# Weight steps in pairs, a shorter centroid chain and a fused softplus end, in another order of issue: clustered attention and a softplus FFN on one core

## The chip, the core and the metric

The kernel runs on one core of one Trainium2 chip. Time is device microseconds (us) of one execution. Before the change three runs gave 818.27, 818.87 and 819.67, so the median is 818.87.

## What is computed

```python
q_assign = np.argmax(np.einsum('bhsd,hcd->bhsc', q_n, c_n), axis=-1)   # nearest of 16 centroids
k_assign = np.argmax(np.einsum('bhsd,hcd->bhsc', k_n, c_n), axis=-1)
mask = q_assign[:, :, :, None] == k_assign[:, :, None, :]
scores = np.where(mask, scale * np.matmul(q, k.transpose(0, 1, 3, 2)), -1000000000.0)
attn = softmax(scores)                     # max, exp, sum, division
x = (attn @ v) as (B * S, H * D)
h = x @ w_in
g = np.maximum(h, 0.0) + np.log1p(np.exp(-np.abs(h)))
return g @ w_out
```

Four batches, 8 heads, 768 positions of 64 numbers; the FFN takes 3072 tokens of 512 through 2048. The weights and the centroids are scaled up by a constant factor. `w_in` and `w_out` come as 64-bit floats; q, k, v and the centroids as 32-bit floats.

## The kernel before

The precision is that of 32-bit floats, and the matrix products run in 16-bit floats: each operand is split in a high part (a cast) and a low part (a subtraction), and three products are added. So nearly every tile passes through a cast and a subtraction on one of three engines: ACT, DVE or POOL.

The work stands in 192 score tiles of 128 queries by 768 keys, numbered t, in eight passes `pi` of 24 tiles (half a batch each). For a tile, `scores(t)` (L1084 on) issues four matmuls into one of two `s` buffers, the row maximum on DVE (L1116), the exponential on ACT (L1125), then cast (L579) and subtraction (L561) into `phl`, and a DMA that transposes a pair of tiles into `pt` (`flip`). The first 24 tiles are transposed by PE instead, in full precision (L1142), since the path by DMA has not started by then. `attend(t)` (L1238, L1242, L1243) multiplies `pt` by v. When all heads of a pass are attended, `ffn1(pi, f)` computes 16 tiles `h` (L1330 to L1332) for that pass, `softplus(pi, f)` turns each of them into g, and `ffn2` multiplies by `w_out` (L1418 to L1420).

`softplus` has five operations for each h: |h| with a sign (L1357 on DVE or L1361 on ACT), max(h, 0) (L1368 or L1369), exp (L1374), log (L1375), and the sum (L1379 on DVE or POOL). The PSUM bank of `h` is given back after the second. Three banks are shared by h (two at most), o (two at most) and x.

`prep_weights(step)` turns 64-bit weights into the two 16-bit parts in 32 steps of 128 by 512, 16 for `w_in` and 16 for `w_out`: a load into a free part of `wo`, a scaling (L707 to L709, on ACT, DVE or POOL), the low bits (L724, L725), two joins on DVE (L736, L742), a cast and a subtraction. `prep_centroids` normalizes the centroids in a chain of small operations (L618 to L639), mostly on DVE, which ends in three transposes on PE and a copy (L644, L647); the first assignment of keys waits for it.

Everything is issued in an order that is written down: `SEQUENCE` names at each position the chain whose next operation is issued, and, by its thousands, on which of the engines open to it. Each engine runs its instructions in that order. Small matmuls on constant data (`warm`, L526) fill places where PE is expected to wait; how many there are is computed from the planner's own costs.

Of the kernel before, what the change touches and what calls it, by code (L numbers as in the profile page):

```python
# [8 lines left out]
F16 = mybir.dt.float16  # L9
# [10 lines left out]
SW2 = 256.0  # L20
# [9 lines left out]
PSC = 1560  # L30
PQS = 1950
# [9 lines left out]
WARM_FROM = 600  # L41
WARM_SHARE = 0.65
# [6 lines left out]
TURN = "...e.t.t................"  # L49
CAPS = {"h": 2, "o": 2, "x": 3}  # L50
# [54 lines left out]
]  # L105
SEQUENCE = [
# [172 lines left out]
class Order:  # L279
# [7 lines left out]
    PIPE = {"PE": 0, "DVE": 82, "ACT": 105, "POOL": 43, "SP": 0}  # L287

    def __init__(self):
        self.free = {"PE": 1800.0, "DVE": 2500.0, "ACT": 2000.0, "POOL": 2700.0, "SP": 1000.0}  # L290
        self.ev, self.blocked, self.active = {}, {}, {}
        self.dma = 0.0
        self.loads = 0
# [117 lines left out]
    def run(self):  # L411
        for code in SEQUENCE:
# [6 lines left out]
            if eng == "PE" and self.warm:  # L419
                self.warm(self.free["PE"], start)  # L420
# [1101 lines left out]
```

## Time and profile before

| | us |
|---|---|
| runs: lowest, median, highest | 818.27, 818.87, 819.67 |
| span of the profiled execution, first to last instruction | 816.3 |
| PE busy | 801.5 (98%) |
| DVE busy | 653.4 (80%) |
| ACT busy | 603.3 (74%) |
| POOL busy | 446.3 (55%) |

Of the profiled execution the page gives the span, which leaves out the launch ahead of the first instruction and what follows the last one; the median of the runs is 2.6 us above it. PE is the TensorE matmul, DVE is VectorE, ACT is ScalarE, POOL is GpSimd; SP issues the DMAs. Busy time is the union of an engine's instructions. Matmuls overlap in the pipeline, so that a short wait of PE can be hidden in its busy time.

### The profile page before, as it was taken

The numbers are of one execution on the slowest core, as the hardware profiler recorded it, in microseconds if no ns is written. First come the engines' busy times: TensorE is split into PE (matmuls) and PEld (weight loads), VectorE is DVE, ScalarE is ACT, GpSimd is POOL, SyncE is SP. The second block draws the span as 40 slices with busy tenths as digits, with TensorE's granted clock in tenths as the row PEclk, the third lists the DMA queues.
The fourth block names the chain that finished last, engine by engine and source line by source line (L and its number), as shares of the span: only waits on it lengthen the run. The fifth ranks groups of instructions, "written<-read, shape, count | busy, mean of one in ns | idle before, by whom it ended". The sixth has DMA issues, their size and how long they took to land.

```text
span 816.3 us, 17689 instructions
## 1 busy us (share of the span) xinstructions
PE 801.5 (98%) x6851; PEld 510.7 (63%) x6851; DVE 653.4 (80%) x1205; ACT 603.3 (74%) x1175; POOL 446.3 (55%) x365
## 2 busy tenths in 40 slices
PE   8999989999999999999999999999999999999998
PEld 8898756665666666665666656656666666555554
DVE  8999999999887887988788898898797877543232
ACT  7999999998777788786777677766787775534330
POOL 4336464565467568675573575765655685432330
DMA  9436999999979999999989799999999777520001
GB/s 331 156 91 158 224 209 255 187 204 215 207 166 166 185 203 204 191 218 180 185 168 179 144 197 181 196 197 188 185 171 164 142 133 140 119 53 14 26 1 39
DMA packets 386451, 134.15 MB, mean 164 GB/s; under 512 B 362688, under 2 KB 379328, under 8 KB 386368
## 3 DMA queue, kind: packets, MB, share of 16 engines
q1 hardware_dynamic: 386368, 133.03, 80.4%
q8 instruction: 53, 0.87, 0.4%
q14 instruction: 30, 0.25, 0.1%
HBM read 35.68 MB, written 6.29 MB: 51 GB/s over the span
## 4 chain that ended last, share of the span: by engine, by line
PE 77%; DMA 7%; DVE 5%; ACT 5%; issue 3%; POOL 2%; SPq 0%; POOLq 0%; ACTq 0%; DVEq 0%
PE s L1100 11%; PE o L1418 9%; PE o L1420 9%; PE o L1419 9%; PE h L1330 9%; PE h L1332 9%; PE h L1331 9%; PE mbank L1242 6%; DMA pt<-phl 5%; PE mbank L1243 3%; PE mbank L1238 2%; ACT p L1125 2%; DVE negm L1116 2%; PE pT L1142 1%; POOL phl L561 1%
## 5 line engine op out<-in xcount | busy, mean ns | idle before, releaser
L1125 ACT ACTIVATE p<-s,negm 128x768 f32<-128x768 f32 x190 | 171.3, 903 | 65.1 <-DVE negm L1116 48.9
L1116 DVE TENSOR_REDUCE negm<-s 128x1 f32<-128x768 f32 x192 | 180.8, 948 | 22.2 <-PE s L1100 21.2
L561 POOL TENSOR_TENSOR phl<-p,phl 128x768 f16<-128x768 f32 x86 | 142.9, 1666 | 76.8 <-ACT phl L579 46.9
L1330 PE MATMUL h<-xT,wi 128*128 128x384 f16 x512 | 166.9, 326 | 0.4 <-ACT fg L1369 0.4
L1332 PE MATMUL h<-xT,wi 128*128 128x384 f16 x512 | 166.9, 326 | 0.0
L1331 PE MATMUL h<-xT,wi 128*128 128x384 f16 x512 | 166.9, 326 | 0.0
L1100 PE MATMUL s<-kt,qt 128*128 128x384 f16 x768 | 155.8, 326 | 2.8 <-ACT p L1125 1.5
L1418 PE MATMUL o<-wo,gh 128*128 128x512 f16 (+2 forms) x392 | 146.5, 375 | 0.8 <-DVE ot L1444 0.6
L1420 PE MATMUL o<-wo,gh 128*128 128x512 f16 (+2 forms) x392 | 146.5, 375 | 0.0
L1419 PE MATMUL o<-wo,gh 128*128 128x512 f16 (+2 forms) x392 | 146.5, 375 | 0.0
L1379 POOL TENSOR_TENSOR fg<-fg,fa 128x384 f32<-128x384 f32 x72 | 77.2, 1074 | 84.4 <-ACT fa L1375 64.4
L1242 PE MATMUL mbank<-vb,pt 128*128 128x128 f16 x1008 | 107.4, 220 | 2.7 <-DVE negm L1116 1.3
L1243 PE MATMUL mbank<-vb,pt 128*128 128x64 f16 x1008 | 103.1, 193 | 0.0
L1100 PEld LDWEIGHTS <-qt 128*128 128x128 f16 x768 | 71.3, 98 | 49.0 <-issue 4.9
L1242 PEld LDWEIGHTS <-pt 128*128 128x128 f16 x1008 | 89.6, 98 | 16.6 <-DMA pt<-phl 4.7
L579 ACT CAST phl<-p 128x768 f16<-128x768 f32 x112 | 91.5, 829 | 11.3 <-DMA pt<-phl 8.3
L1361 ACT ACTIVATE fa<-h 128x384 f32<-128x384 f32 x93 | 45.4, 489 | 70.1 <-PE h L1332 54.0
L1243 PEld LDWEIGHTS <-pt 128*128 128x128 f16 x1008 | 87.6, 98 | 11.4
L561 DVE TENSOR_TENSOR phl<-p,phl 128x768 f16<-128x768 f32 x76 | 81.5, 1078 | 3.0 <-ACT phl L579 2.3
L561 POOL TENSOR_TENSOR gh<-fg,gh 128x768 f16<-128x768 f32 x38 | 65.7, 1728 | 17.0 <-DVE gh L579 7.7
L1332 PEld LDWEIGHTS <-wi 128*128 128x128 f16 x512 | 50.1, 98 | 33.2
L1331 PEld LDWEIGHTS <-wi 128*128 128x128 f16 x512 | 50.1, 98 | 32.4 <-issue 0.5
(182 smaller groups left out, 1388.6 us busy)
## 6 DMA issues: line engine op xcount, KB each, us to landing
wo<-in_moe_w_in_dram SPq DMA_DIRECT2D x16, 512.0 KB, 6.4
wo<-in_moe_w_out_dram SPq DMA_DIRECT2D x14, 512.0 KB, 4.4
rawk<-in_k_dram SPq DMA_DIRECT2D x16, 384.0 KB, 4.3
rawq<-in_q_dram SPq DMA_DIRECT2D x16, 384.0 KB, 4.3
rawv<-in_v_dram SPq DMA_DIRECT2D x16, 384.0 KB, 4.3
out_dram<-ot SPq DMA_DIRECT2D x23, 256.0 KB, 2.4
pt<-phl SPq DMA_TRANSPOSE x82, 5.9
wraw<-in_moe_w_out_dram SPq DMA_DIRECT2D x2, 512.0 KB, 4.6
```

The lines of the kernel that those rows point to most:

```text
L561: [lambda e=e: e.tensor_tensor(dst, a, b, ALU.subtract) for e in (nc.gpsimd, nc.vector)],
L1100: nc.tensor.matmul(st[:, j, :SH], qt[:, s, i], kt[:, s, NT // 2 * j : NT // 2 * (j + 1)], start=(s == 0), stop=(s == 1),)
L1116: yield op("DVE", 950, lambda: nc.vector.tensor_reduce(negm, st[:, :, :SH], AX.XY, ALU.max, negate=True))
L1125: yield op("ACT", 1000, lambda: nc.scalar.activation(ex, st[:, :, :SH], AF.Exp, bias=negm, accum_out=total))
L1242: nc.tensor.matmul(av, pt[:, 0, c], vb[:, c, : 2 * D], start=(c == 0), stop=False)
L1243: nc.tensor.matmul(av[:, D:], pt[:, 1, c], vb[:, c, D : 2 * D], start=False, stop=(c == NT - 1))
L1330: nc.tensor.matmul(hp, w[0], x[0], start=(c == 0), stop=False)
L1331: nc.tensor.matmul(hp, w[0], x[1], start=False, stop=False)
L1332: nc.tensor.matmul(hp, w[1], x[0], start=False, stop=(c == NP - 1))
L1418: nc.tensor.matmul(out_, g[0], wo[:, f, 0, 0, side], start=(f == f0), stop=False)
L1419: nc.tensor.matmul(out_, g[0], wo[:, f, 0, 1, side], start=False, stop=False)
L1420: nc.tensor.matmul(out_, g[1], wo[:, f, 0, 0, side], start=False, stop=(f == f0 + NF // 2 - 1))
```

## The change

- Weight steps: 14 pairs of steps (all of `w_in`, twelve of `w_out`) work on 128 by 1024 at a time; four single steps of `w_out` stay. `wi` is laid out so that the two parts of a pair lie side by side. The rooms into which raw weights are loaded are given out in pairs.
- The scaling on POOL has a second operand (`1.0, mult, mult`) in place of `None`, here and at `prep_q`; the planner's cost for it is lower (`PSC`, `PQS`).
- Centroids: squares and their sum in one ACT instruction, one round of Newton's step for the square root in place of two, the 0.5 and the 1e-6 in one instruction, the two copies in one and the two differences in one, the clearing of `cb` on a chain of its own.
- `FUSED = 2`: in the first two passes max(h, 0) and the sum are one DVE instruction that reads `h` from PSUM after the log; `h`'s bank is given back after it.
- Half of the `ot` scalings may go to ACT; banks are picked from the front of the list of idle ones.
- Fillers stand in a table (`FILLS`, 149 of them, all within the first 171 positions of the order) in place of the computed ones (206).
- Another `SEQUENCE` and other ranks.

```diff
-PSC = 1560
-PQS = 1950
+PSC = 660
+PQS = 920
...
+FUSED = 2
...
+FILLS = {
+    11: 33, 18: 10, 28: 14, 36: 10, 46: 3, 50: 2, 64: 10, 87: 11, 88: 6, 100: 4, 113: 5, 117: 11, 120: 10, 141: 7,
+    159: 6, 165: 3, 170: 4,
+}
+
 SEQUENCE = [
-    0, 0, 0, 0, 0, 0, 0, 0, 0, 0, 1, 2, 4, 0, 1, 0, 6, 468, 469, 1001, 0, 468, 0, 0, 3, 1, 468, 2004, 1, 0, 468, 1,
...
-        bank = min(self.idle, key=self.ev.get)
+        bank = self.idle[0]
...
-            if eng == "PE" and self.warm:
-                self.warm(self.free["PE"], start)
+            if at in FILLS:
+                self.warm(FILLS[at])
...
+    def warm(count):
+        for _ in range(count):
+            nc.tensor.matmul(idle, eye, ones[:, :WARM], start=True, stop=True)
...
-        yield either(300, 250, lambda e: e.tensor_tensor(sq, cf, cf, ALU.mult))
-        yield dve(lambda: V.tensor_reduce(ss, sq, AX.X, ALU.add))
-        yield dve(lambda: V.tensor_scalar(sg, ss, 1e-30, None, ALU.max))
-        yield op("ACT", 200, lambda: nc.scalar.activation(nrm, sg, AF.Ln))
-        yield op("ACT", 200, lambda: nc.scalar.activation(nrm, nrm, AF.Exp, scale=0.5))
-        for _ in range(2):
...
+        yield op("ACT", 370, lambda: nc.scalar.activation(sq, cf, AF.Square, accum_out=ss))
+        yield op("ACT", 200, lambda: nc.scalar.activation(nrm, ss, AF.Ln, bias=tiny))
+        yield op("ACT", 200, lambda: nc.scalar.activation(nrm, nrm, AF.Exp, scale=0.5))
+        yield dve(lambda: V.reciprocal(rn, nrm))
+        yield dve(lambda: V.scalar_tensor_tensor(nrm, rn, ss, nrm, ALU.mult, ALU.add))
+        yield dve(lambda: V.tensor_scalar(nrm, nrm, 0.5, 1e-6, ALU.mult, ALU.add))
+        yield dve(lambda: V.reciprocal(rn, nrm))
+        yield dve(lambda: V.tensor_scalar(cn, cf, rn, None, ALU.mult), 235, shared=True)
...
-    wi = cpool.tile([P, DM // P, DFF // WC, 2, WC], F16, name="wi")
+    wi = cpool.tile([P, DFF // WC, DM // P, 2, WC], F16, name="wi")
...
+    groups = [(s, 2) for s in range(0, NWI + 12, 2)] + [(s, 1) for s in range(NWI + 12, NWI + NF)]
...
-            (660, 420, PSC),
+            (240 + 435 * n, 145 + 275 * n, 130 + 530 * n),
...
-                lambda: nc.gpsimd.tensor_scalar(mag, val, sc, None, ALU.mult),
+                lambda: nc.gpsimd.tensor_scalar(mag, val, sc, 1.0, ALU.mult, ALU.mult),
...
-        yield op("DVE", 685, join, shared=True)
+        yield op("DVE", 151 + 534 * n, join, shared=True)
...
+        fused = pi < FUSED
+        if not fused:
+            yield op(
+                ("DVE", "ACT"),
...
+            od.drop(hk)
         yield op("ACT", 520, lambda: nc.scalar.activation(a, a, AF.Exp, scale=sign[0]))
         yield op("ACT", 520, lambda: nc.scalar.activation(a, a, AF.Ln, bias=1.0))
...
+        if fused:
+            yield op("DVE", 560, lambda: nc.vector.scalar_tensor_tensor(g[:, f % 2], hp, 0.0, a, ALU.max, ALU.add))
+            od.drop(hk)
+        else:
...
```

What the order makes of it is shown at two places. The first is the start of DVE, from the first instruction on the centroids on (`css` is the sum of squares, `cnrm` the norm, `crn` its inverse, `cb` the copies for the transposes, `kn` and `qn` the split keys and queries). Before:

```order
L618 TENSOR_TENSOR csq<-cf 128x64
L619 TENSOR_REDUCE css<-csq 128x1
L620 TENSOR_SCALAR csg<-css 128x1
L624 RECIPROCAL crn<-cnrm 128x1
L625 SCALAR_TENSOR_TENSOR cnrm<-crn,csg,cnrm 128x1
L626 TENSOR_SCALAR cnrm<-cnrm 128x1
L624 RECIPROCAL crn<-cnrm 128x1
L625 SCALAR_TENSOR_TENSOR cnrm<-crn,csg,cnrm 128x1
L626 TENSOR_SCALAR cnrm<-cnrm 128x1
L627 TENSOR_SCALAR cnrm<-cnrm 128x1
L561 TENSOR_TENSOR kn_0_141<-rawk_120,kn_0_141 128x12x64
L628 RECIPROCAL crn<-cnrm 128x1
```

And in the changed kernel, DVE from the same place:

```order
L625 RECIPROCAL crn<-cnrm 128x1
L626 SCALAR_TENSOR_TENSOR cnrm<-crn,css,cnrm 128x1
L627 TENSOR_SCALAR cnrm<-cnrm 128x1
L628 RECIPROCAL crn<-cnrm 128x1
L629 TENSOR_SCALAR cn<-cf,crn 128x64
L634 CAST cb<-cn 128x128
L635 TENSOR_TENSOR cb<-cn,cb 128x2x64
L553 TENSOR_TENSOR kn_0_182<-rawk_123,kn_0_182 128x12x64
```

Seven small instructions now make the whole chain on DVE, and it ends ahead of the first subtraction for the keys; before, that subtraction and two others stood inside it.

The second place is ACT at the first h tile, `h_0`, of the first pass (`fa` holds |h| and then the log, `fg` holds g, `s` and `phl` are score tiles). Before:

```order
L1361 ACTIVATE fa_0_1951<-h_0_1937 128x384
L725 ACTIVATE wo<-wo,down 128x512
L1369 ACTIVATE fg_0_1952<-h_0_1937 128x384
L1374 ACTIVATE fa_0_1951<-fa_0_1951 128x384
L1187 CAST phl_3_1989<-s_3_1830 128x768
L1375 ACTIVATE fa_0_1951<-fa_0_1951 128x384
L579 CAST wo<-wo 128x512
L1187 CAST phl_3_1989<-s_4_1909 128x768
L579 CAST wo<-wo 128x512
```

In the changed kernel, ACT from the first tile's exp on, and DVE from its |h| on:

```order
L1377 ACTIVATE fa_0_1804<-fa_0_1804 128x384
L1378 ACTIVATE fa_0_1804<-fa_0_1804 128x384
L1362 ACTIVATE fa_1_1878<-h_1_1806 128x384
L1377 ACTIVATE fa_1_1878<-fa_1_1878 128x384
L1127 ACTIVATE p_2_5_1869,sum_1_1738<-s_5_1854,negm_5_1863 128x768
L1378 ACTIVATE fa_1_1878<-fa_1_1878 128x384
```

```order
L1358 TENSOR_SCALAR fa_0_1804<-h_0_1779 128x384
L1046 TENSOR_REDUCE aq_1_1848<-sim_q_1_1639 128x12
L1261 TENSOR_REDUCE x_0_1_1772<-mbank 128x128
L1190 TENSOR_TENSOR phl_3_1815<-s_4_1781,phl_3_1815 128x768
L1118 TENSOR_REDUCE negm_5_1863<-s_5_1854 128x1
L1380 SCALAR_TENSOR_TENSOR fg_0_1805<-h_0_1779,fa_0_1804 128x384
```

Exp and log now follow each other on ACT, max(h, 0) is gone from it, and the weight steps' instructions no longer stand among them; on DVE the one fused instruction comes five places behind the |h|.

## Rows read from the trace of the kernel before

**Rows 1.** The page: span, and busy us (share of span) xinstructions of each engine.

```profile
span 816.3 us, 17689 instructions
PE 801.5 (98%) x6851; PEld 510.7 (63%) x6851; DVE 653.4 (80%) x1205; ACT 603.3 (74%) x1175; POOL 446.3 (55%) x365
```

**Rows 2.** Stretches: length, busy PE, PEld, DVE, ACT, POOL; PE clock, DMA share, GB/s.

```profile
0.00:21.70 21.70, 18.57 (x354) 17.82 (x355) 18.14 (x77) 17.40 (x29) 10.63 (x18) 1.00 0.93 337
21.70:88.00 66.30, 65.15 (x653) 57.32 (x651) 65.62 (x135) 65.75 (x137) 30.32 (x30) 1.00 0.51 143
88.00:147.00 59.00, 53.68 (x505) 38.02 (x504) 57.50 (x102) 58.38 (x115) 30.77 (x25) 1.00 1.06 219
147.00:816.00 669.00, 664.13 (x5345) 397.58 (x5345) 512.16 (x895) 461.80 (x898) 374.57 (x293) 1.00 0.81 156
```

**Rows 3.** Groups by line and form: the fillers in 21.7 to 88 and in 88 to 147.

```profile
L526 PE MATMUL mbank<-ones,eye 128*128 128x120 f16 x40 | 3.1, 216 | 0.0
...
L526 PE MATMUL fill<-ones,eye 128*128 128x120 f16 x29 | 2.0, 216 | 0.0
```

**Rows 4.** Waits of PE and its weight loads in 88 to 147: us, times, longest.

```profile
PE s L1100 <- ACT p L1125: 1.3, 3, 0.8
...
PEld L1242 <- DMA pt<-phl: 1.7, 1, 1.7
```

**Rows 5.** Timeline of the opening: first, last DVE instruction on centroids, and ACT's copy.

```profile
2.69 0.23 DVE L618 TENSOR_TENSOR csq<-cf 128x64 f32<-128x64 f32 x1 [0.91 <-DMA cf<-in_centroids_dram]
...
8.91 0.21 DVE L639 TENSOR_TENSOR cb<-cn,cb 128x64 f16<-128x64 f32 x1
...
10.44 0.48 ACT L647 COPY cents<-centsT 128x384 f16<-128x384 f16 x1
```

**Rows 6.** Groups by line and form, whole span: weight steps, and DVE casts of two sizes.

```profile
L736 DVE SCALAR_TENSOR_TENSOR wo<-wo 128x512 int32<-128x512 int32 x30 | 20.5, 700 | 0.5 <-issue 0.4
...
L725 ACT ACTIVATE wo<-wo,down 128x512 int32<-128x512 uint16 x21 | 16.3, 784 | 0.0
...
L579 DVE CAST gh<-fg 128x768 f16<-128x768 f32 x14 | 7.8, 555 | 0.7 <-POOL fg L1379 0.3
...
L579 DVE CAST xn<-x 128x384 f16<-128x384 f32 x10 | 3.7, 365 | 0.2
```

**Rows 7.** The same view: max(h, 0) and the sum in softplus.

```profile
L1379 POOL TENSOR_TENSOR fg<-fg,fa 128x384 f32<-128x384 f32 x72 | 77.2, 1074 | 84.4 <-ACT fa L1375 64.4 <-DVE fg L1368 17.3 <-DVE phl L561 1.7
...
L1369 ACT ACTIVATE fg<-h 128x384 f32<-128x384 f32 x82 | 40.0, 487 | 20.2 <-DVE fa L1357 15.1 <-POOL gh L561 5.1
...
L1379 DVE TENSOR_TENSOR fg<-fg,fa 128x384 f32<-128x384 f32 x56 | 36.3, 652 | 9.3 <-ACT fa L1375 9.1
...
L1368 DVE TENSOR_SCALAR fg<-h 128x384 f32<-128x384 f32 x46 | 25.3, 551 | 13.8 <-ACT fa L1361 11.6 <-POOL gh L561 2.0
```

**Rows 8.** The same view: the low part of a score tile on POOL and on DVE.

```profile
L561 POOL TENSOR_TENSOR phl<-p,phl 128x768 f16<-128x768 f32 x86 | 142.9, 1666 | 76.8 <-ACT phl L579 46.9 <-DVE phl L579 27.6 <-POOL kn L561 0.9
...
L561 DVE TENSOR_TENSOR phl<-p,phl 128x768 f16<-128x768 f32 x76 | 81.5, 1078 | 3.0 <-ACT phl L579 2.3 <-POOL phl L579 0.2
...
L1188 DVE TENSOR_TENSOR phl<-s,phl 128x768 f16<-128x768 f32 x2 | 1.8, 946 | 0.0
```

**Rows 9.** The same view: POOL's cast of weights, and its one scaling with a constant.

```profile
L579 POOL CAST wi<-wo 128x512 f16<-128x512 f32 x5 | 4.0, 801 | 10.0 <-DVE wo L742 8.6 <-ACT ptf L552 1.4
...
L1047 POOL TENSOR_SCALAR n<-n 128x96 f16<-128x96 f16 x2 | 1.2, 582 | 3.1 <-DVE live L1042 3.1
```

**Rows 10.** First h tile's max and sum; PE's waits for h; h's matmuls in 106 to 154.

```profile
109.96 0.48 ACT L1369 ACTIVATE fg<-h 128x384 f32<-128x384 f32 x1
...
114.26 0.99 POOL L1379 TENSOR_TENSOR fg<-fg,fa 128x384 f32<-128x384 f32 x1
...
L1330 PE MATMUL h<-xT,wi 128*128 128x384 f16 x512 | 166.9, 326 | 0.4 <-ACT fg L1369 0.4
...
L1330 PE MATMUL h<-xT,wi x41: 323/326/327, 106.8 to 153.7; 128*128 128x384 f16 x41
```

More of the change, by code (lines that the diff above doesn't have):

```diff
@@ L289, in __init__ @@
     def __init__(self):
-        self.free = {"PE": 1800.0, "DVE": 2500.0, "ACT": 2000.0, "POOL": 2700.0, "SP": 1000.0}
+        self.free = {"PE": 1800.0, "DVE": 2500.0, "ACT": 2650.0, "POOL": 2700.0, "SP": 1000.0}
         self.ev, self.blocked, self.active = {}, {}, {}
@@ L411, in run @@
     def run(self):
-        for code in SEQUENCE:
+        for at, code in enumerate(SEQUENCE):
             which, seq = divmod(code, 1000)
@@ L517, in tile_cluster_attention__then__softplus_ffn @@
     idle = mbank[:, 512 - WARM :]
-    def warm(begin, end):
-        ready, spot = min([(od.ev[b], b[1]) for b in od.idle] + [(od.mread, 9)])
-        gap = end - max(begin, ready)
-        if gap > (150 if begin < 30000 else WARM_FROM):
-            out = idle if spot == 9 else ps_u.tile([P, 512], F32, tag=f"u{spot}", name="fill")[:, :WARM]
-            for _ in range(int(gap * (0.95 if begin < 2500 else 0.75 if begin < 30000 else WARM_SHARE) / (100 if begin < 2500 else 52))):
-                nc.tensor.matmul(out, eye, ones[:, :WARM], start=True, stop=True)
+    def warm(count):
+        for _ in range(count):
+            nc.tensor.matmul(idle, eye, ones[:, :WARM], start=True, stop=True)
     od.warm = warm
@@ L607, in tile_cluster_attention__then__softplus_ffn @@
     cents = cpool.tile([P, 3, H, NCL], F16, name="cents")
+    tiny = cpool.tile([P, 1], F32, name="tiny")
+    nc.vector.memset(tiny, 1e-30)
     def prep_centroids():
         sq = p2.tile([P, D], F32, tag="x320", name="csq", bufs=1)
-        small = [cpool.tile([P, 1], F32, name=f"c{nm}") for nm in ("ss", "sg", "nrm", "rn")]
-        ss, sg, nrm, rn = small
+        small = [cpool.tile([P, 1], F32, name=f"c{nm}") for nm in ("ss", "nrm", "rn")]
+        ss, nrm, rn = small
         V = nc.vector
@@ L631, in prep_centroids, with blank_cb @@
         cn = p2.tile([P, D], F32, name="cn", **own(keys[0], 2))
-        yield dve(lambda: V.tensor_scalar(cn, cf, rn, None, ALU.mult), shared=True)
-        od.set(cf_key)
-        cb = p2.tile([P, 3, 2, D], F16, name="cb", **own(keys[1], 2))
-        yield either(195, 330, lambda e: e.memset(cb, 0.0))
-        for j in range(2):
-            yield either(195, 240, lambda e, j=j: e.tensor_copy(cb[:, 0, j], cn))
-        yield either(195, 290, lambda e: e.tensor_tensor(cb[:, 1, 0], cn, cb[:, 0, 0], ALU.subtract))
-        yield either(195, 290, lambda e: e.tensor_tensor(cb[:, 2, 1], cn, cb[:, 0, 0], ALU.subtract))
+        cb = p2.tile([P, 3, 2, D], F16, name="cb", **own(keys[1], 2))
+        def blank_cb():
+            yield either(195, 330, lambda e: e.memset(cb, 0.0))
+            od.set(("cb",))
+        od.spawn(blank_cb(), od.cur["prio"])
+        yield op("ACT", 370, lambda: nc.scalar.activation(sq, cf, AF.Square, accum_out=ss))
[6 more added lines that the diff above has]
+        yield dve(lambda: V.tensor_scalar(cn, cf, rn, None, ALU.mult), 235, shared=True)
+        od.set(cf_key)
+        both = cn.unsqueeze(1).to_broadcast([P, 2, D])
+        rest = cb.rearrange("p a j d -> p (a j) d")[:, 2:6:3]
+        yield wait("cb")
+        yield either(260, 330, lambda e: e.tensor_copy(cb[:, 0], both))
+        yield either(260, 430, lambda e: e.tensor_tensor(rest, both, cb[:, 0], ALU.subtract))
         hk, ps = yield from bank("x", False, [P, 3, P], F16, "centsT")
@@ L696, in prep_weights @@
         if step:
-            yield wait("wd", step - 1)
-        if f >= 0 and f // 2 in rooms:
-            yield wait("wr", rooms[f // 2])
+            yield wait("wd", groups[gi - 1][0])
+        if f >= 0:
+            for last in sorted({rooms[r] for r in range(f // 2, (f + n - 1) // 2 + 1) if r in rooms}):
+                yield wait("wr", last)
         gate = int(WGATE + step * WPACE)
@@ L744, in prep_weights @@
         )
-        yield cast(part[:, 0], val, WC, WBIAS)
-        yield sub(part[:, 1], val, part[:, 0], WC)
-        od.set(("wr", step))
+        yield cast(part[:, :, 0], val, n * WC, WBIAS)
+        yield sub(part[:, :, 1], val, part[:, :, 0], n * WC)
+        for k in range(n):
+            od.set(("wr", step + k))
         if key:
@@ L1051, in prep_q @@
             ("POOL", "DVE"),
-            (180 + 1290 * part, 130 + DQA * part),
+            (480 + 990 * part, 130 + DQA * part),
             [
@@ L1124, in scores @@
         total = sums[n // 2, pi][:, n % 2 * nt + i]
[L1125 removed]
+        yield op("ACT", 980, lambda: nc.scalar.activation(ex, st[:, :, :SH], AF.Exp, bias=negm, accum_out=total))
         if kind(t) == ".":
@@ L1327, in emit @@
                 for c in range(2 * half, 2 * half + 2):
-                    w = [wi[:, c, f * P // WC, s, w0 : w0 + P] for s in range(2)]
+                    w = [wi[:, f * P // WC, c, s, w0 : w0 + P] for s in range(2)]
                     x = [xT[pi][:, c, s] for s in range(2)]
@@ L1363, in softplus @@
         yield op(("DVE", "ACT"), (550, 485), (minus_abs, plus_abs), bias=ABIAS)
[L1364 to L1373 removed]
+        fused = pi < FUSED
+        if not fused:
+            yield op(
+                ("DVE", "ACT"),
+                (550, 485),
+                (
+                    lambda: nc.vector.tensor_scalar(g[:, f % 2], hp, 0.0, None, ALU.max),
+                    lambda: nc.scalar.activation(g[:, f % 2], hp, AF.Relu),
+                ),
+                bias=RBIAS,
+            )
+            od.drop(hk)
         yield op("ACT", 520, lambda: nc.scalar.activation(a, a, AF.Exp, scale=sign[0]))
         yield op("ACT", 520, lambda: nc.scalar.activation(a, a, AF.Ln, bias=1.0))
[L1376 to L1382 removed]
+        if fused:
+            yield op("DVE", 560, lambda: nc.vector.scalar_tensor_tensor(g[:, f % 2], hp, 0.0, a, ALU.max, ALU.add))
+            od.drop(hk)
+        else:
+            yield op(
+                ("DVE", "POOL"),
+                (550, 1000),
+                [lambda e=e: e.tensor_tensor(g[:, f % 2], g[:, f % 2], a, ALU.add) for e in (nc.vector, nc.gpsimd)],
+                shared=True,
+                bias=GBIAS,
+            )
         od.set(ak)
@@ L1435, in store @@
         if half == 0:
-            yield op("DVE", 680, lambda: nc.vector.tensor_scalar(acc, po, 1.0 / SW2, None, ALU.mult))
+            yield op(
+                ("DVE", "ACT"),
+                (680, 595),
+                (
+                    lambda: nc.vector.tensor_scalar(acc, po, 1.0 / SW2, None, ALU.mult),
+                    lambda: nc.scalar.activation(acc, po, AF.Copy, scale=1.0 / SW2),
+                ),
+            )
             od.drop(ok)
@@ L1476, in tile_cluster_attention__then__softplus_ffn @@
         od.spawn(attend(t), t + LAG)
-    for step in range(len(wsteps)):
-        od.spawn(prep_weights(step), WGATE + WDUE + step * WPACE)
+    for gi in range(len(groups)):
+        od.spawn(prep_weights(gi), WGATE + WDUE + groups[gi][0] * WPACE)
     firsts = []
```

76 lines of the change are left out of this document (27 added, 49 removed), and 329 rows, old and new, of the table SEQUENCE.

## Prediction

> **What bounds the kernel now.** First the page: PE is busy in 801.5 of 816.3 us, DVE in 653.4, ACT in 603.3, POOL in 446.3 [rows 1]. PE does the same useful matmuls after the change, so what can be won is PE's idle time and its fillers, and they must be placed. The table by stretches does that [rows 2]; I cut it at 21.7 us, where the first score matmul starts, at 88, where PE's rate sags, and at 147, where it recovers. Idle time of PE is 21.70 - 18.57 = 3.1 us in the opening, 66.30 - 65.15 = 1.2 up to 88, 59.00 - 53.68 = 5.3 up to 147, and 669.00 - 664.13 = 4.9 in all the rest, of which the last store behind the last matmul is the larger part. Fillers take another 3.1 us of 21.7 to 88 and 2.0 of 88 to 147 [rows 3]. The clock is 1.00 throughout [rows 2], so fillers are worth nothing beyond keeping it there.
>
> So there are three pieces to win: the opening, whose 21.7 us are mostly latency; 1.2 + 3.1 = 4.3 us up to 88; 5.3 + 2.0 = 7.3 us up to 147. After 147 PE is the bound and a change has nothing to give, only something to lose.
>
> Who holds PE up in the two middle stretches? DVE is busy for 65.62 of 66.30 and 57.50 of 59.00 us, ACT for 65.75 and 58.38, POOL for 30.32 and 30.77 [rows 2]. Two engines are full, one is half empty. The waits of PE agree: it waits for ACT's exponential, 1.3 us in three waits, and its weight load for the transposed tile, 1.7 us in one [rows 4]. In this piece elementwise work sets the pace, and PE's idle time is the remainder.
>
> **The change, part by part.** Opening. The chain on the centroids begins at 2.69 us, its last DVE instruction starts at 8.91, and ACT's copy starts at 10.44 [rows 5]. The order takes three DVE instructions out at the front (one on ACT now), three of a second Newton round and one constant, a memset, a copy and a difference: ten, at 0.21 to 0.23 by the two shown [rows 5] and less for the narrow ones, so 1.5 to 2.3 us of chain; and three large subtractions no longer stand inside it. The assignment of the first keys can so begin some 2 us earlier. But the keys behind the first ones, ACT's copies and POOL stay where their loads put them, and POOL now has more to do in the opening (casts and subtractions of later keys). Bounds: 0 if the loads decide, 2.9 if everything behind moves up with DVE, which is the sum of the DVE durations that the new order has less ahead of the first score tile. I take 1.8, nearer to DVE's end, because DVE is busy in 18.14 of these 21.70 us [rows 2], almost without a hole once the keys have landed.
>
> Weight pairs. What an instruction costs beyond its elements shows in one DVE form at two sizes: 555 ns for 768 and 365 for 384, so 2 x 365 - 555 = 175 ns [rows 6]. A join of a pair is then estimated at 2 x 700 - 175 = 1225 ns, ACT's low bits at 2 x 784 - 175 = 1393. The bounds are one single (a pair for the price of one) and two singles (nothing won). A pair saves 175 ns twice on DVE for sure and four times on whichever engine does the rest, 1.05 us in all; 14 pairs save 15 us, spread over three engines.
>
> Fused softplus. In passes 0 and 1, 32 tiles, max(h, 0) goes (487 ns on ACT or 551 on DVE) and the sum goes (1074 on POOL or 652 on DVE) [rows 7]; one DVE instruction over 384 comes, priced like max(h, 0) from PSUM at 551, bounded by 652 above.
>
> Moved work. Over the whole order DVE's subtractions for score tiles go from 76 to 58, ACT's casts for them from 112 to 90, and POOL takes 18 of each. A subtraction costs 1666 ns on POOL against 1078 on DVE [rows 8].
>
> The sum for the middle is made over the piece of the order that holds the matmuls PE did from 77 to 152 us. On DVE there: 20 single joins become 8 of a pair and 2 single, 20 x 0.70 - 8 x 1.225 - 2 x 0.70 = 2.8 us less; three max(h, 0) and six sums go, 3 x 0.55 + 6 x 0.65 = 5.6 less; subtractions for score tiles fall from 9 to 4, 5.4 less; 11 fused ones come, 6.1 more; the rest (one more row maximum, one more subtraction for g) is some 2 more. DVE has 5.7 us less. ACT has nine max(h, 0) less, 4.4 us, and by the pairs and moved casts another us or so. POOL gets about 10 us more, on 30.77 of 59 busy. With DVE as full as before, the piece is shorter by what DVE loses: 5.7, bounded below by 0 (POOL late instead) and above by PE's 7.3. I take 4.5 for 88 to 147, since a fifth of such a saving should stay as idle time of DVE at places where its input is late. Up to 88 DVE loses less (the pairs of `w_in`, against more row maxima taken early): 1.5, between 0 and 4.3.
>
> After 147. POOL gets in all some 70 us more (18 subtractions at 1.67, 18 casts of score tiles and 18 of g at 0.8 [rows 9] or a little more, then keys and values), DVE and ACT less. PE's idle time there can only grow; I charge 0.3. Fewer fillers in the table (149 against 206) are the 57 that stood behind the opening; they cost nothing more than is already counted. The loads move as many bytes in fewer issues.
>
> One rule of the skill speaks against moving work to POOL. The row first: the same subtraction on DVE costs 946 ns with one input in PSUM and 1078 with both in SBUF [rows 8]. The Trainium skill, "SBUF — State Buffer", section "Who interferes with whom", says that a DVE instruction with two SBUF inputs and a POOL instruction that reads SBUF exclude each other for their whole length. By the trace the loss is (1078 - 946) x 76 = 10 us of DVE over the run, small against its 653.4, and with 58 of them left it falls to 7.7 even at the old rate; by the rule, POOL's extra work would have to fit beside DVE's without overlap, which is a rival below.
>
> Sum: 1.8 + 1.5 + 4.5 - 0.3 = 7.5 us. The span goes from 816.3 to 808.8. The runs' median stands 2.6 above the span (818.87 against 816.3), so 811.4.
>
> **Rivals.**
> PE becomes the bound everywhere. For it: ACT and DVE both get lighter and POOL was half idle. Against: DVE keeps nine tenths of its work in the middle. It gives 2.9 + 4.3 + 7.3 = 14.5, so 804.4.
>
> POOL and DVE exclude each other. In the middle piece POOL's 40 us become 51, and DVE's instructions with two SBUF inputs, about 17, become 9: 60 of some 66 us must go one by one. For it: POOL's subtraction takes 1666 ns however it is placed, so one that starts first holds a DVE one back by more than its own length. Against: DVE has fewer of them. Then casts and subtractions come late, the 6 us of the middle are lost, and PE, idle for 4.9 us after 147, idles some 3 us more: 816.3 - 1.8 + 3.0 = 817.5 of span, 820.1. (This is the rule of the Trainium skill named above at full strength.)
>
> The bank of h is held longer; this ends on the slower side. The first h tile's bank was free at 110.44, after max(h, 0); the sum ended at 115.25, 4.8 us later [rows 10], and the bank is now held until an instruction at that place. From the first matmul at 106.8 the old order would make that hold 8.5 us. Ten tiles, of four of that line's matmuls each, take 106.8 to 153.7 [rows 10], 4.7 us a tile, and with two banks PE waits once a hold exceeds two of these, 9.4. At 12 us, one more queue like the first tile's, each of the ten adds (12 - 9.4) / 2 = 1.3, 13 us, which eats the 7.5 and leaves 824.4. For it: only two banks, and PE hardly waits for h now (0.4 us [rows 10]), so nothing shows the margin. Against: the new order puts exp and log next to each other and the fused instruction soon behind, so a hold is little more than its own four instructions.
>
> POOL's scaling is dear. No row shows it on 512 or 1024 elements. Its cast of 512 takes 801 ns; its one scaling takes 582 ns for 96 elements [rows 9], 6.1 per element. The ten new ones are between 1.4 us (two casts less 0.2) and 6.2 us each. I take 1.4, as the cast has the size and the memory of a weight step. At 6.2, the six ahead of 147 us would add 29 us to POOL where 28 are free, weights come late, and half of it shows: about 825.
>
> The change doing less than it says would be pairs at twice the price: 1.05 us a pair comes back, and about 2 us of the gain with it; it lies in the range.
>
> **How the numbers follow.** 811.4 with its own bounds has 0.58; PE as the bound 0.14; POOL against DVE 0.13; the bank 0.08; POOL's scaling 0.07. The range 804.5 to 818.5 takes in the first two but for a tail, and part of the third. A measurement of this kernel tells 0.2%, 1.6 us. Faster by more: 0.56 of the forecast, the 0.14, and a tenth in the others that the opening pays for, 0.80. The same: 0.08. Slower: 0.12.
>
> **What would show it.** The first score matmul near 20 us in place of 21.7; PE idle below 3 us in the stretch that was 88 to 147, with DVE still above 95% and ACT clearly below its 99%; POOL above 60% there; joins of 1024 near 1.2 us; scalings on POOL near 1.4 us. The forecast is wrong if PE waits for the fused instruction ahead of h, if PE's idle time after the middle grows past 8 us, or if DVE's subtraction rises well above 1078 ns.

## The result: slower by 0.9%, and the profile after

The changed kernel took 826.83 us (median of 823.38, 826.68, 826.98 and 828.82) against 819.27 of four runs of the kernel before beside it: a ratio of 1.0088, 95% interval 1.0065 to 1.0110. Forecast were 811.4 us, in a range up to 818.5. The profiled execution, at 823.38, is the fastest of the four; `changed_again`, below, adds the profile of one at 827.55.

The page of the changed kernel, first execution, and then the same two lines for the execution in `changed_again`:

```profile
span 821.5 us, 17416 instructions
...
PE 801.4 (98%) x6794; PEld 508.8 (62%) x6794; DVE 658.3 (80%) x1120; ACT 559.8 (68%) x1079; POOL 549.6 (67%) x424
```

```profile
span 825.7 us, 17416 instructions
...
PE 803.5 (97%) x6794; PEld 510.9 (62%) x6794; DVE 660.4 (80%) x1120; ACT 560.7 (68%) x1079; POOL 549.2 (67%) x424
```

Against [rows 1], DVE has 85 instructions less and is busy 5 us more. ACT has lost 43.5 us, POOL has gained 103.3. The stretches of the changed kernel, first execution (columns as in [rows 2]):

```profile
0.00:21.70 21.70, 18.82 (x358) 17.81 (x359) 16.35 (x69) 16.06 (x26) 13.85 (x22) 1.00 0.93 334
21.70:88.00 66.30, 64.79 (x625) 56.86 (x622) 65.09 (x102) 62.74 (x119) 42.79 (x31) 1.00 0.47 139
88.00:147.00 59.00, 52.47 (x486) 36.29 (x486) 57.84 (x93) 52.13 (x91) 39.81 (x27) 1.00 1.08 225
147.00:816.00 669.00, 663.27 (x5310) 396.29 (x5308) 518.18 (x859) 428.87 (x846) 453.14 (x345) 1.00 0.82 156
```

In 88 to 147 ACT is free for 7 of 59 us now, but DVE is still full (57.84), so the piece does not get shorter. After 147 us DVE's busy time has risen from 512.16 to 518.18 us with 36 instructions fewer. What they cost shows in the groups by line and form: DVE's low part of a score tile, its low part of g, its small sum `rs` ahead of the division and its joins of pairs; then POOL's low part of a score tile:

```profile
L553 DVE TENSOR_TENSOR phl<-p,phl 128x768 f16<-128x768 f32 x58 | 70.0, 1210 | 8.6 <-ACT phl L571 4.4 <-POOL phl L571 2.4 <-POOL phl L553 1.4
...
L553 DVE TENSOR_TENSOR gh<-fg,gh 128x768 f16<-128x768 f32 x26 | 31.6, 1214 | 4.1 <-POOL gh L571 2.8 <-ACT gh L571 1.3
...
L1272 DVE TENSOR_SCALAR rs<-sum 128x6 f32<-128x6 f32 x32 | 14.6, 455 | 0.0
...
L737 DVE SCALAR_TENSOR_TENSOR wo<-wo 128x1024 int32<-128x1024 int32 x11 | 14.2, 1297 | 0.1
...
L743 DVE SCALAR_TENSOR_TENSOR wo<-wi,wo 128x1024 int32<-128x1024 int32 x8 | 9.6, 1222 | 0.3
...
L743 DVE SCALAR_TENSOR_TENSOR wo<-wo 128x1024 int32<-128x1024 int32 x6 | 8.6, 1431 | 0.1
```

```profile
L553 POOL TENSOR_TENSOR phl<-p,phl 128x768 f16<-128x768 f32 x104 | 184.2, 1777 | 56.0 <-ACT phl L571 31.9 <-DVE phl L571 19.2 <-DVE negm L1118 1.4
```

In the kernel before, the low part of a score tile took 1078 ns on DVE and 1666 on POOL [rows 8], the low part of g and `rs` on DVE:

```profile
L561 DVE TENSOR_TENSOR gh<-fg,gh 128x768 f16<-128x768 f32 x26 | 27.1, 1042 | 9.7 <-POOL gh L579 5.8 <-ACT gh L579 3.8
...
L1271 DVE TENSOR_SCALAR rs<-sum 128x6 f32<-128x6 f32 x32 | 9.5, 297 | 0.0
```

One place in the timeline of the changed kernel shows why:

```profile
306.12 1.64 POOL L553 TENSOR_TENSOR phl<-p,phl 128x768 f16<-128x768 f32 x1
306.48 2.10 DVE L553 TENSOR_TENSOR phl<-p,phl 128x768 f16<-128x768 f32 x1
```

DVE's subtraction starts 0.36 us into POOL's and takes what is left of POOL's (1.28) and then 0.82. Of the 58 subtractions of this form, 26 start while POOL runs nothing that reads SBUF; each of them takes 0.92 to 0.96 us. The 32 that start during a POOL instruction that reads SBUF take 1.45 (median), 2.23 at most. An instruction of DVE that takes one of its inputs from PSUM does not care: the fused one takes 0.547 beside such a POOL instruction (27 of them) and 0.545 otherwise.

Two inputs from SBUF are not the only case. DVE's cast of a score tile, from SBUF to SBUF, takes 0.93 us beside such a POOL instruction (8 of them) and 0.55 otherwise, and `rs` 0.50 (19) and 0.16; the reciprocal on the same small tile takes 0.19 in either case.

By the Trainium skill, "SBUF — State Buffer", section "Who interferes with whom", a DVE instruction with two SBUF inputs contends with a GpSimd instruction that reads SBUF, not with one that only writes it, and the port pair that the two share is an exclusive lock. The trace agrees: 1.45 against 0.95, and 0.547 against 0.545 where one input is in PSUM.

PE's waits in the changed kernel, whole span, show no single new culprit:

```profile
PE s L1102 <- ACT p L1127: 3.9, 8, 0.9
...
PE h L1331 <- DVE fg L1380: 0.8, 1, 0.8
```

To place the loss I add up PE's useful matmuls in order of start (each at the time its form takes when PE isn't kept waiting, fillers at nothing) and note how long each kernel takes from one amount of that work to the next; all finish 12.6 or 12.7 us after the 770th. The work from 59 to 124 us is the piece on which the prediction's sum for the middle was made.

| us of time for this part of PE's work | 0 to 17 | 17 to 59 | 59 to 124 | 124 to 770 |
|---|---|---|---|---|
| before (span 816.3) | 34.0 | 42.8 | 74.9 | 652.0 |
| changed, first execution (821.5) | 32.7 | 44.1 | 75.9 | 656.1 |
| `changed_again` (825.7) | 36.6 | 44.1 | 76.1 | 656.2 |
| `changed_late_weights` (825.2) | 34.1 | 44.1 | 77.0 | 657.2 |
| `changed_pool_blind` (817.6) | 35.3 | 43.9 | 73.6 | 652.1 |
| `before_pool_blind` (818.2) | 35.4 | 42.8 | 74.7 | 652.7 |

So the changed kernel loses 1.3 us ahead of the middle, 1 us in it and 4 after it, and its opening is better than before once and worse once.

### The profile page after: what moved, and what is told of

Its sections match the earlier page's. It is cut to its first block, busy times and chain, and to the rows that moved or that the text cites. A ratio compares the mean times of both kernels' runs of the same rounds, so it can differ in the third digit from the quotient of the medians.

```text
span 821.5 us, 17416 instructions
## 1 busy us (share of the span) xinstructions
PE 801.4 (98%) x6794; PEld 508.8 (62%) x6794; DVE 658.3 (80%) x1120; ACT 559.8 (68%) x1079; POOL 549.6 (67%) x424
## 4 chain that ended last, share of the span: by engine, by line
PE 60%; DVE 18%; DMA 10%; POOL 5%; ACT 4%; issue 3%; SPq 0%; DVEq 0%; POOLq 0%; ACTq 0%
PE s L1102 9%; PE o L1425 7%; PE o L1427 7%; PE o L1426 7%; DMA pt<-phl 7%; PE h L1331 7%; PE h L1333 7%; PE h L1332 7%; PE mbank L1243 4%; DVE negm L1118 3%; PE mbank L1244 2%; POOL phl L553 2%; ACT p L1127 2%; DVE phl L553 1%; DVE wo L737 1%
## 5 line engine op out<-in xcount | busy, mean ns | idle before, releaser
L553 POOL TENSOR_TENSOR phl<-p,phl 128x768 f16<-128x768 f32 x104 | 184.2, 1777 | 56.0 <-ACT phl L571 31.9
L1386 POOL TENSOR_TENSOR fg<-fg,fa 128x384 f32<-128x384 f32 x60 | 67.4, 1128 | 68.6 <-ACT fa L1378 65.7
L1244 PE MATMUL mbank<-vb,pt 128*128 128x64 f16 x1008 | 103.3, 193 | 0.0
L571 ACT CAST phl<-p 128x768 f16<-128x768 f32 x90 | 73.6, 829 | 13.7 <-DMA pt<-phl 12.1
L1362 ACT ACTIVATE fa<-h 128x384 f32<-128x384 f32 x89 | 43.2, 487 | 57.9 <-PE h L1333 47.4
L553 POOL TENSOR_TENSOR gh<-fg,gh 128x768 f16<-128x768 f32 x38 | 65.9, 1736 | 17.2 <-DVE gh L571 11.2
L553 DVE TENSOR_TENSOR phl<-p,phl 128x768 f16<-128x768 f32 x58 | 70.0, 1210 | 8.6 <-ACT phl L571 4.4
L1377 ACT ACTIVATE fa<-fa 128x384 f32<-128x384 f32 x128 | 66.4, 522 | 15.3 <-DVE fa L1358 14.5
L1332 PEld LDWEIGHTS <-wi 128*128 128x128 f16 x512 | 50.1, 98 | 36.1 <-issue 3.0
```

Of the source, the lines that this page charges most:

```text
L553: [lambda e=e: e.tensor_tensor(dst, a, b, ALU.subtract) for e in (nc.gpsimd, nc.vector)],
L1244: nc.tensor.matmul(av[:, D:], pt[:, 1, c], vb[:, c, D : 2 * D], start=False, stop=(c == NT - 1))
L1332: nc.tensor.matmul(hp, w[0], x[1], start=False, stop=False)
```

## The experiments

The theory after the result: POOL's added work locks DVE's two-input instructions out (and they it), so DVE's saved instructions are paid back. This is called the lock below. Rivals: POOL is only a longer queue; the new order of PE, DVE and banks is worse in itself; the pairs, the held bank of h, or the fillers cost it. Ratios are to the kernel before, run beside each.

**Is it POOL, and is it the reading?**

`casts_to_act`: in `run`, casts of score tiles and g that the order gives to POOL go to ACT.

```diff
+            if which == 2 and opt.get("home") is not None:
+                which = opt["home"]
...
-            yield cast(phl[:, u, 0], p32, S)
+            yield cast(phl[:, u, 0], p32, S, home=0)
```

> The changed kernel, its order kept, but the 50 casts of score tiles and the 32 of g that stood on POOL are done by ACT in the same places (about 78 us of busy time leave POOL, 68 come to ACT). Theory (POOL and DVE lock each other): DVE's low part of a score tile falls from 1210 to about 1120 ns, its low part of g from 1214 to about 1080, the small sum for the division (rs) from 455 to about 330, the last h tiles' waits go, and the time comes to 819 to 823 us. Rival (the new order of PE, DVE and the banks is itself worse): DVE's durations fall too, but the time stays at 825 to 828. Rival (POOL is only late as a queue): the time falls to 819 to 823 as well, with DVE's durations where they were, near 1210.

867.35 us, 1.0600 (1.0572 to 1.0628): far outside every expectation. PE now waits 17.2 us for the exponential, as the moved casts stand ahead of it on ACT:

```profile
PE s L1105 <- ACT p L1130: 17.2, 19, 2.5
```

DVE's subtraction stayed at 1201 ns, where the theory had 1120, and its `rs` fell to 259. It decides nothing between the theories; it shows that a place in this order is worth more than the engine's busy share (ACT is busy for 72% here).

`pool_reads_more` and `pool_writes_more`: the kernel before, with more work on POOL.

```diff
+            if eng == "POOL":
+                self.pools += 1
+                if self.pools > 78 and self.pools % 6 == 0:
+                    self.junk()
...
+        nc.gpsimd.tensor_tensor(room.rearrange("p (c d) -> p c d", d=64), a, b, ALU.subtract)
```

```diff
+        for _ in range(2):
+            nc.gpsimd.memset(room, 0.0)
```

> The kernel before, with 46 more instructions on POOL, one behind every sixth of its own from 150 us on: each subtracts two constants of SBUF and writes 704 elements that nobody reads, about 1.4 us each, 64 us in all, what the change adds to POOL in this stretch (79 us). Theory (lock): DVE's low part of a score tile goes from 1078 to 1150 ns or more, its rs from 297 to 380 or more, and the time rises by 3 to 8 us, to 822 to 827. Rival (POOL late as a queue only): the time rises by as much, but DVE's durations stay at 1078 and 297. Rival (the order of the change alone): PE is the bound after 147 us and POOL has room; within 1 us of before, 818.5 to 820.

> The same 46 places in the kernel before, with two clearings of the same 704 elements on POOL in place of the subtraction: the same time on POOL within a tenth, but nothing is read. Theory (lock by reading): DVE's durations stay at 1078 and 297, and the time rises by less than half of what the reading instructions cost, 819 to 821 us. Rival (POOL late as a queue only): the same rise as with the reading instructions. Rival (the order of the change alone): no rise in either.

Reading: 850.24 us, 1.0387 (1.0373 to 1.0402). Writing only: 834.72, 1.0205 (1.0188 to 1.0221). From the groups of the one and the other:

```profile
L538 POOL TENSOR_TENSOR room<-ones 128x704 f16<-128x704 f16 x46 | 77.1, 1675 | 0.0
...
L573 DVE TENSOR_TENSOR phl<-p,phl 128x768 f16<-128x768 f32 x76 | 95.6, 1263 | 5.2 <-POOL phl L591 2.2 <-ACT phl L591 2.2 <-issue 0.4
```

```profile
L538 POOL MEMSET room<- 128x704 f16 x92 | 63.9, 694 | 2.6
...
L573 DVE TENSOR_TENSOR phl<-p,phl 128x768 f16<-128x768 f32 x76 | 88.1, 1164 | 5.2 <-ACT phl L591 3.4 <-POOL phl L591 1.2 <-issue 0.2
```

Both runs cost far more than any expectation had, and both theories hold half. 64 us of mere writing cost 16 us, though in the kernel before PE hardly waits after 147 us and POOL is idle for almost half the span: a queue that is only longer can cost time, as POOL's own items come later. Reading costs 32, twice as much, with 77 us on POOL. Beside a clearing, DVE's subtraction takes 0.95 us as if alone (7 of the 8 that start during one, here 0.07 us into it; the eighth runs into POOL's next subtraction). Its mean rose to 1164 ns all the same, since 25 of the 76 start beside a reading instruction now, and 20 did before:

```profile
217.06 1.42 POOL L538 MEMSET room<- 128x704 f16 x2
217.13 0.95 DVE L573 TENSOR_TENSOR phl<-p,phl 128x768 f16<-128x768 f32 x1
```

`changed_pool_blind` and `before_pool_blind`: POOL's subtractions, casts and softplus sums wait for the same inputs and keep their length, but read one element of a row only and clear the rest. Their results are left out so.

```diff
-            [lambda e=e: e.tensor_tensor(dst, a, b, ALU.subtract) for e in (nc.gpsimd, nc.vector)],
+            (
+                lambda: dull(2, dst, 2.0**-12, (lambda o, x, y: nc.gpsimd.tensor_tensor(o, x, y, ALU.subtract), dst, a, b)),
+                lambda: nc.vector.tensor_tensor(dst, a, b, ALU.subtract),
+            ),
```

> The changed kernel, with POOL's subtractions, casts and softplus sums taken out: each is done for the first element of a row alone (so it waits for the same inputs), and the rest is a clearing to a constant, twice for a subtraction or a sum, once for a cast, which takes as long within a tenth but reads nothing. The low parts, high parts and sums that POOL would compute are left out so. Theory (lock): DVE's low part of a score tile falls to 950 to 980 ns, its rs below 100, and with the waits gone the time is 806 to 815 us; less than 1 us above the kernel before under the same edit. Rival (POOL late as a queue, or the order itself): the time falls by less than 4 us, and stays 4 to 8 us above the kernel before under the same edit.

> The kernel before under the same edit: POOL's subtractions, casts and softplus sums are left out but for one element of a row, and clearings of the same length stand in their place. Theory (lock): it gains as well, but less than the changed kernel, since POOL reads for 446 us and not for 550: 814 to 818 us. Rival: 818 to 819.5, no gain, since PE is the bound after 147 us.

Changed: 819.03 us, 1.0007 (0.9994 to 1.0019). Before: 819.27, 1.0005 (0.9995 to 1.0016). This decides. POOL is as busy as ever (544.7 us against 549.2), the order is the changed one, and with the reading gone the changed kernel falls by 7.5 us, to the time of the kernel before. That one does not move, where the theory had it gain as well. After 147 us, changed and then before:

```profile
147.00:816.00 669.00, 665.22 (x5342) 398.30 (x5340) 476.79 (x865) 430.46 (x847) 449.37 (x893) 1.00 0.83 157
```

```profile
147.00:816.00 669.00, 664.34 (x5351) 398.10 (x5348) 490.81 (x897) 463.24 (x901) 382.68 (x790) 1.00 0.81 156
```

DVE loses 41 us of busy time there (518.18 to 476.79) in the changed kernel and 21 in the one before: the lock took that much, and in the order of before it fell into DVE's idle time. By the table above the changed kernel gets back 2.5 us in the middle and 4.1 after it (`changed_again` against `changed_pool_blind`). The expected 806 to 815 was too low: after 147 us PE has no more than 3.8 us of idle time left, and in the middle DVE is full even without the lock (70.75 of 73.7 us in the piece that is shown with the step that failed).

**Is it a part of the change?**

`pairs_as_singles`: each operation on a pair is issued twice, for one step each, in the same place.

> The changed kernel, where every operation on a pair of weight steps is issued as two of 128 by 512 behind each other, in the same places, on the same engines. Theory (lock; the pairs are no part of the loss): the time gets worse by at most 2 us, 826 to 829, and all of that before 150 us; the loss after 240 us stays. Rival (an instruction of 1.2 to 2.4 us blocks what waits behind it, and that is the loss): the time falls to 820 to 824.

837.37 us, 1.0231 (1.0217 to 1.0245), slower than either expectation. The pairs are worth 10.8 us in this order; DVE is busy for 671.6 us in place of 660.4.

`changed_unfused`: max(h, 0) and the sum are apart again.

```diff
+                if fused:
+                    nc.scalar.activation(g[:, f % 2], hp, AF.Relu)
...
-            yield op("DVE", 560, lambda: nc.vector.scalar_tensor_tensor(g[:, f % 2], hp, 0.0, a, ALU.max, ALU.add))
+            yield op("DVE", 560, lambda: nc.vector.tensor_tensor(g[:, f % 2], g[:, f % 2], a, ALU.add))
```

> The changed kernel, where the one instruction at the end of softplus in the first two passes is taken apart again: max(h, 0) on ACT right behind the |h| (32 more at 487 ns on ACT), and where the fused instruction stood, a sum on DVE from SBUF, 650 to 780 ns against 548. h's bank is so free some instructions earlier. Theory (the longer hold of the bank costs nothing, the rest is lock): 827 to 831, a little slower, by ACT and DVE. Rival (the bank is held too long in the middle): 821 to 825.

841.38 us, 1.0283 (1.0269 to 1.0297), again slower than either expectation: the bank's rival falls, and the fused instruction is worth 14.8 us here, far more than its count. Part of that can be ACT's, which has 32 instructions more; the two were not taken apart. The sums that stand in its place read SBUF twice:

```profile
L1388 DVE TENSOR_TENSOR fg<-fg,fa 128x384 f32<-128x384 f32 x32 | 31.4, 980 | 6.7 <-ACT fa L1386 6.7
```

980 ns against 548 with `h` in PSUM, 13.8 us of DVE over 32.

`before_with_chain`: the shorter chain on the centroids alone, in the old places.

> The kernel before with its own order and only the shorter chain on the centroids, issued in the places of the old one (squares and sum on ACT in one instruction, one Newton round, one copy, one difference; the rest of the places empty). Theory (the loads of the keys, landing at 7 to 10 us, decide the opening): 817.5 to 819.5, no change that can be told. Rival (the chain holds the first assignment up, as the forecast had it): 816 to 817.5.

818.26 us, 0.9996 (0.9987 to 1.0005). DVE has 3.3 us less to do, and the first score matmul starts at 21.91 in place of 21.71.

`before_with_pairs` and `before_with_both` put pairs into the order of before (in both, part of the FFN's weights comes out changed, so they count for work and order alone).

> The kernel before with its own order, where 12 pairs of weight steps (seven of the eight of w_in, five of w_out) work on 128 by 1024: the pair is issued in the places of one of the two steps, the other's places stay empty; the loads stay single. 24 joins at 700 ns on DVE give way to 12 (two per pair) at 1225, and as much goes on the other engines. Theory (the pairs are worth their count where DVE is full, up to 152 us): about 5 us less work on DVE, and 814 to 817 us. Rival (a pair's later start or longer hold costs what it saves in an order that was not made for it): 818 to 821.

> The kernel before with its own order, the 12 pairs and the shorter chain. Theory (the new order, with POOL's larger share, is what loses): 813 to 816.5, faster than both kernels. Rival (the parts do not pay in the old order): 818 to 821.

838.44 us, 1.0245 (1.0231 to 1.0259), and 837.64, 1.0226 (1.0205 to 1.0247). Inconclusive: the piece from 59 to 124 us of PE's work loses 17 us in the one and 12 in the other, and the piece ahead of it 4 in either, where pairs stand in places meant for single steps. What pairs would bring with an order of their own and POOL as it was is not shown.

**Clock, opening, and the small sum.**

> The changed kernel as it is, beside the others on one chip. Its profiled execution was 823.4 us with the clock granted at 1.00, its other three 826.7 to 828.8 us with mean clocks of 0.993 to 0.998. Theory (a part of the loss is TensorE's clock, which falls where PE now stands idle without fillers, at 11 to 15 us or at 95 to 110): a run at 826 or more shows a stretch of some 5 us at half clock there. Rival (the clock falls at random anywhere): no such place.

826.57 us, 1.0093 (1.0078 to 1.0107). In its opening the clock fell:

```profile
11.00:15.00 4.00, 2.13 (x47) 1.96 (x46) 3.73 (x12) 2.33 (x3) 4.00 (x6) 0.82 1.04 393
15.00:19.00 4.00, 4.00 (x68) 4.00 (x66) 3.80 (x9) 2.01 (x3) 1.64 (x2) 0.50 1.05 389
```

PE was busy for 2.13 of 4 us and then ran at 0.50, which is 1.2 GHz. So it looked as if fillers were missing.

`guard_fillers` adds 78 to the table; these are the new entries.

```diff
+    52: 14, 66: 12, 502: 8, 521: 7, 533: 16, 535: 8, 544: 5, 553: 8,
```

> The changed kernel with 78 more small matmuls on constants: 26 in the opening, ahead of the two places where PE waits between 11 and 15 us, and 52 ahead of the six where it waits between 95 and 105 us (the kernel before has 29 there). Theory (clock): the granted clock is 1.00 in every run, and the median falls to 823 to 824.5, what the best run of the changed kernel shows; what is left above before, some 4.5 us, is something else. Rival (the clock is not the cause of the higher runs): 826 to 829, as without.

828.88 us, 1.0131 (1.0118 to 1.0144), with the mean clock at 0.998 to 1.000. The clock is not the loss: keeping it this way cost 2.3 us more than not, and the first execution of the changed kernel loses its 5 us at 1.00.

`changed_no_rs` and `before_no_rs` divide by the sum alone.

> The changed kernel without the small sum ahead of the division (rs, 32 instructions of 6 elements a row on DVE, 455 ns each, 14.6 us): 1e-9 is left out of the divisor, which is at least 1. Theory (lock): these 32 do next to no work of their own, their time is waiting for POOL, and each stands between the last matmul of a head pair and its softplus work; DVE falls to about 646 us, and the time by 2 to 5 us, to 821.5 to 824.5. Rival (DVE's time after 147 us costs nothing, since PE is the bound there): 825.5 to 827.

> The kernel before under the same edit (32 instructions of 297 ns, 9.5 us of DVE). Theory (lock): in this kernel PE hardly waits after 147 us and the instructions cost 160 ns each up to 152 us; 817 to 819. Rival (they cost as they do in the changed kernel): 814 to 817.

826.34 us, 1.0089 (1.0074 to 1.0104), and 817.97, 0.9994 (0.9986 to 1.0003): no change in either, though DVE is busy for 13 us less in the changed kernel. The rival was right here: these 32 do not carry the loss. By the count of PE's work the middle does get 1.6 us shorter than in `changed_again`, but the part behind it 2.2 longer.

`changed_opening` moves the low part of the third pair of keys to DVE; `changed_opening_no_rs` does both.

```diff
-    ... 1456, 1455, 456, 455, 2, 5, 5, 7, 7, 2, ...
+    ... 1456, 1455, 456, 455, 2, 5, 5, 1007, 7, 2, ...
```

> The changed kernel with one instruction moved: the low part of the third pair of keys, 1.64 us on POOL behind two casts and a clearing, goes to DVE in the same place of the order (about 0.95 us). PE waited 1.9 us for it in the opening of the last run of the changed kernel, and its clock fell to half right after. Theory (POOL in the chain of the first keys is why the opening is some 3 us late and the clock falls there): the first score matmul comes 1.5 to 3 us earlier than in that run, the clock stays at 1.00, and the time is 823 to 825. Rival (the landing of the keys decides alone): 825.5 to 827.5.

> Both edits together on the changed kernel. Theory: they act in different places, so their gains add: 819 to 822. Rival: no more than the better of the two.

826.70 us, 1.0097 (1.0081 to 1.0113), and 825.80, 1.0083 (1.0070 to 1.0097). The rivals hold.

`changed_late_weights` issues the first two loads of weights behind the last loads of values; `changed_late_weights_all` has all three edits.

> The changed kernel with two loads issued later: the first two pairs of weights (1 MB each; the kernel before loads 0.5 MB at a time) go out behind the last two loads of values instead of ahead of them, so that they share no time with the keys. Seven runs of the changed kernel and its variants show the second pair of keys taken up by DVE between 7.4 and 9.3 us and the first score matmul between 21.8 and 25.7; before and its variants take that pair up at 7.0 to 7.6 us, with one at 9.4. Theory (the new order of loads makes the keys land late): the second pair is taken up by 8 us, the first score matmul comes by 23, the clock stays near 1.00, and the time is 822.5 to 825. Rival (the keys land as they do anyway, the rest of the chain is what is late): first score matmul at 24 to 25, 825.5 to 827.5.

> The same, with the third pair of keys' low part on DVE and without the small sum rs as well. Theory (loads): with the keys there in time the instruction moved to DVE pays too; 821 to 824. Rival: 825 to 827, since neither edit changed the time by itself.

826.87 us, 1.0101 (1.0083 to 1.0119), and 825.55, 1.0093 (1.0077 to 1.0109). The first half of the theory came nearly true: the second pair of keys is taken up at 7.53 us, the first score matmul starts at 23.23 (expected by 23), the profile's clock is 1.00, and PE is through its first 17 us of work at 34.1, as in the kernel before (34.0). The time did not follow: the middle took 0.9 us more and the rest 1.0 more than in `changed_again`. So with an opening like that of before the changed kernel still loses 1.3, 2.1 and 5.2 us in the three parts behind it.

No version here beats the kernel before by more than can be told.

## Why the prediction was wrong, step by step

The step that failed is the sum for the middle, which had DVE do 5.7 us less and took nothing for the lock. DVE was busy there for 1.1 us more, and the lock cost the changed kernel 7.5 us in all. The rest of the miss is gains that were not there even without the lock: with POOL blind the four parts of the table stand at +1.3, +1.1, -1.3 and +0.1 us against the kernel before, where -1.8, -1.5, -4.5 and +0.3 were forecast (only the middle is cut as in the prediction, the other parts lie near its stretches).

The piece of the middle in the kernel before, in the changed one, and in `changed_pool_blind` (columns as in [rows 2]):

```profile
76.70:151.70 75.00, 69.32 (x656) 50.89 (x655) 73.31 (x130) 73.88 (x144) 38.79 (x32) 1.00 1.04 229
```

```profile
76.70:152.70 76.00, 67.95 (x627) 49.27 (x626) 74.36 (x116) 66.66 (x117) 49.26 (x35) 1.00 0.99 213
```

```profile
79.10:152.80 73.70, 68.65 (x627) 50.31 (x626) 70.75 (x115) 66.23 (x117) 50.24 (x83) 0.98 1.00 219
```

- **The opening** (-1.8): failed. The chain on the centroids was not what the first tile waits for. Alone it gained nothing, which was the lower bound ("0 if the loads decide"); I took a value near the other end because DVE was nearly full there, but its work was not what was waited for. In the change the opening is 1.3 us better once and 2.6 worse once, with a fall of the clock in it; with POOL blind it is 1.3 us worse, at a mean clock of 0.92 up to 21.7 us.
- **Up to 88** (-1.5): failed; 17 to 59 us of PE's work takes 1.3 us more, and 1.1 more with POOL blind, so the lock is not why. Why is not shown.
- **The middle** (-4.5): DVE was to have 5.7 us less in the piece; it went from 73.3 us with 130 instructions to 74.4 with 116. By groups: the low parts of score tiles -3.8, four fewer of 0.95 us, where five of 1.08 stood; softplus +0.6 (counted: +0.5); the joins -1.45 where -2.8 stood; the assignments of keys and queries, of which some 31 instructions stand in the piece against 20, about +4 where "the rest" had 2; and the `rs`, 4 in either, +2.2 where nothing stood. A join of a pair took 1365 ns in this piece, 1223 with POOL blind: the estimate of 1225 was right for a DVE left alone. Without the lock DVE's work in the piece falls by 2.6 us, to 70.75, and the piece by 1.3: the count of the order was too good by itself.
- **After 147** (+0.3): mis-sized worst, 4.1 to 5.2 us. "PE is the bound" was read from its idle time of 4.9 us, and taken to mean that POOL had room. The clearings show that 64 us on POOL can cost 16 there even without a lock. In the changed order it was the lock: with POOL blind this part takes 652.1 us, as before (652.0). POOL's share was mis-sized too, 78.6 us more after 147 us and 103.3 in all, where some 70 stood.
- **The lock** was priced from means: "(1078 - 946) x 76 = 10 us of DVE over the run". A mean hides that an instruction either meets nobody or takes some 0.5 us more, and that POOL's extra work raises the number that meet (32 of 58 against 20 of 76): 15 us for this form alone, where 7.7 was thought to be left. It also hides that other forms are lengthened too, and that in the middle DVE is full. The rival that POOL and DVE exclude each other had the right cause, 0.13 of the chances, and 820.1 us: it put the middle's gain at nothing and the loss after it at 3.0, and kept the gain of the opening, which did not exist.
- **The other rivals.** The bank of h: PE waits 0.8 us once for the fused instruction, and unfusing costs 14.8, so no. POOL's scaling on 1024 takes 1.12 to 1.23 us, 1.4 was taken, 6.2 feared. Fewer fillers were to cost nothing more: more of them did not help, by `guard_fillers`.
- **The signs named in advance** spoke clearly: DVE's subtraction at 1210 (1078 was the mark) and PE's idle time in 88 to 147 at 6.5 us where below 3 was asked. The other two signs of being wrong were faint: PE waited once, 0.8 us, for the fused instruction, and its idle time after 147 us is 5.7 us, where 8 was the mark.

## What to carry to other kernels

Before work is moved to POOL, list which of DVE's instructions read SBUF twice, add its casts and scalar sums from SBUF to SBUF, and count how many will run beside it: their price is not their mean but a meeting, some 0.5 us here for 768 elements, and it shows in the time where DVE has no idle time to hide it. An instruction that takes one input from PSUM can be worth more than its count says, as it meets nobody. In an order fitted to its engines to the tenth of a microsecond, an engine that is idle half the time need not have room; look at what its own items are waited for.

## What was not expected

The same lock took 21 us of DVE's time after 147 us in the kernel before, and taking it away brought nothing; in the changed kernel it took 41, and 7.5 us of the whole time. Casts that added 61 us to an engine busy for 68% cost 41 us of time. And the opening's time is not passed on: an opening 2.5 us shorter ended at the same time. Which of DVE's instructions carry the lock's cost to PE stays open; the `rs`, each of which waits longest for its size, do not by themselves. Why the part from 17 to 59 us got longer stays open as well.
